# A causal convolution and an ELU feed-forward on one core: wider convolution bands, and the last output accumulators split by token block

## The chip, the cores and the metric

The kernel runs on one core of a Trainium2 chip. The metric is the time of one execution on the device in microseconds (us); the number given is the median over several executions.

## The reference

Everything is computed for 8 x 4096 = 32,768 tokens of 192 channels. First comes a causal convolution over 7 tokens with one set of softmaxed taps per head (8 heads of 24 channels), then a feed-forward block of width 2048 whose activation is ELU.

```python
w = softmax(weight)                      # (8 heads, 7 taps)
x_pad = concat([zeros(B, 6, D), x], 1)   # causal: six zeros ahead of each sequence
att[b,s,h,:] = sum_k w[h,k] * x_pad[b, s+k, head h]
h = att @ w_in                           # (32768,192) @ (192,2048)
g = where(h > 0, h, exp(min(h, 0)) - 1)  # ELU
out = g @ w_out                          # (32768,2048) @ (2048,192)
```

## The kernel before

**Tiling.** The tokens are taken in 32 superblocks of 1024 (`SUP`), each of two groups `g` of 512 tokens (`GS`). The hidden width is cut in 16 blocks `q` of 128 (`FC`). TensorE is used as two independent halves of 64 rows each: `rt = 0` holds contraction rows 0 to 63 and `rt = 1` holds rows 64 to 127 (`tile_position=(HP * rt, 0)`). The document calls them the lower and the upper half. All eight PSUM banks are one tile `H` of 8 x 512 fp32 columns, and every accumulator takes one bank.

**Three kinds of matmul.**

- *Convolution* (`"c"`, L968). The stationary operand is a band matrix `Tm` for one head, the moving operand is a window of raw x (`xg`, 240 columns: 10 windows of 24 channels). A window has 112 output tokens (`CW`), so the band is read as `Tm[rows, h, 0:CW]`, though the tile is 128 columns wide (`BW`). A superblock has 4 units `m` of two heads; each unit needs two matmuls in the lower half (64 rows) and, after those, two in the upper half (54 rows) that add to the same bank. ScalarE then copies the unit to `csb` (L735), and a DMA transpose on the SP queue (L587) makes `att`, the next superblock's moving operand.
- *First product* (`"h"`, L993). For each `q` and group three matmuls of 512 columns with `w_in` stationary fill a bank. The lower half computes group 0, the upper half group 1. The bank then goes through three engines: ScalarE writes the exp to `E` (L739), GpSimd takes the minimum with 1 (L692), and VectorE computes max(E - 1, H) and writes the fp16 block `gT` (L855). The bank is free when VectorE is done (`s_tt`).
- *Second product* (`"o"`, L1016). `gT` is stationary, 64 rows x 128 tokens, and `w_out` moves 192 columns. The accumulator for a half superblock `k` and group `g` holds two blocks `kb` of 128 tokens side by side in one bank (384 columns). The two halves of TensorE add to it in turns (`s_turn`); after the last turn (`s_fin`) ScalarE copies 384 columns to `osb` (L746), and a store of 192 KB is issued on the SP queue (L544). The very last one, `(NK - 1, 1)`, is copied by VectorE (L846) and stored from ScalarE's queue (L748).

**What sets the order.** Each engine runs one list in order. A planner in the kernel's Python (L95 to L379) writes TensorE's order before the program is built: it keeps one clock per half and adds fixed costs to it (`MM_H`, `MM_O`, `MM_C = 216.0, 82.5, 102.5` ns). A new accumulator takes the bank whose modelled `freed` time is the earliest (`take_bank`, L121). The orders of ScalarE, VectorE and of SP's stores follow from the same plan. GpSimd's order is that of the units, with two x loads per superblock (`load_x`, issue at L608) put in front of certain minima.

**The end.** After the last first product, only second products are left. The planner writes them as `tail` (L334 to L354). In a first pass (`second == 0`) the lower half works for group 0 and the upper for group 1; in the second pass they change places. Each pass goes through k = 62 and k = 63, which are the two halves of the last superblock. Both groups of k = 63 therefore end at the same time, with the last matmuls of the program.

Of the kernel before, what the change touches and what calls it, by code (L numbers as in the profile page):

```python
# [12 lines left out]
P = 128  # L13
HP = 64
FC = 128
D = 192
# [3 lines left out]
CW = 112  # L20
GS = 512
SUP = 2 * GS
# [43 lines left out]
def bass_lightweight_conv__then__act_elu_kernel(  # L66
# [18 lines left out]
    NS = NT // SUP  # L85
    SPB = S // SUP
    NP = NS * NQ
    NK = 2 * NS
    assert SPB > NXB and min(O_AT) + NB > NQ

    x_flat = x.rearrange("b s d -> (b s) d")
# [63 lines left out]
    def o_items(k, g, rt, qs, visit, first, final):  # L155


        todo = [(q, kb) for q in qs for kb in range(2)]

        def issue(i):  # L160
            q, kb = todo[i]
            take_bank(("a", k, g), rt)
            if modelled():
                t = NQ * (k // 2) + q
                clock[rt] = max(clock[rt], gt_at[t, g], turned.get((k, g), 0.0) if first and i == 0 else 0.0)
            starts, ends = first and i == 0, final and i == len(todo) - 1
            item = ("o", k, g, rt, q, kb, visit if starts else None, ends)
            plan.append((clock[rt] - AHEAD, item))
            if ends:
                visits[k, g] = visit + 1  # L170
                turned[k, g] = clock[rt] + MM_O + TURNS

        gate = lambda: visits.get((k, g), 0) == visit
        return [(MM_O, lambda i=i: issue(i), gate) for i in range(len(todo))]
# [160 lines left out]
    for second in range(2):  # L335
        for rt in range(2):
            g = rt ^ second
            k, b = divmod(NP - O_AT[g], NB)
            late = NQ - QB
            if second == 0:  # L340
                lead = TAIL - (late - QB * b)
                for kk, q0, q1, v, first in (
                    (k, QB * b, late, 2 * b, True),
                    (k + 1, 0, lead, 0, True),
                    (k, late, NQ, 2 * b, False),
                    (k + 1, lead, NQ, 0, False),
                ):
                    tail[rt] += o_items(kk, g, rt, range(q0, q1), v, first, not first)
            else:
                for kk, q0, v in ((k, QB * b, 2 * b), (k + 1, 0, 0)):  # L350
                    tail[rt] += evacuated(
                        o_items(kk, g, rt, range(q0, NQ), v + 1, True, True), kk, g
                    )
# [45 lines left out]
    with ExitStack() as stack:  # L399
# [139 lines left out]
            return att[:, 0, j, c0:c1], H[:, b, c0:c1]  # L539

        def out_group(eng, k, g):
            t, half = divmod(k, 2)
            row = SUP * t + GS * g + 2 * P * half
            eng.dma_start(  # L544
                out[row : row + 2 * P, :].rearrange("(k p) d -> p k d", p=P),
                osb[:, k % 2, g, :, :],
            ).then_inc(s_out[k % 2], 16)

        def conv_evac(W, m):

# [12 lines left out]
        def acc_of(k, g):  # L563
            return H[:, bank_of["a", k, g], :]
# [6 lines left out]
                W(s_oev[g], [a for a in act_order if a[0] == "e" and a[2] == g].index(("e", k, g)) + 1)  # L571

        def out_evac(W, k, g):
            W(s_out[k % 2], 32 * (k // 2))
            W(s_fin[g], k + 1)
            return (
                osb[:, k % 2, g, :, :].rearrange("p k d -> p (k d)"),
                acc_of(k, g)[:, 0 : 2 * D],
            )

        def transpose(eng, W, s):
# [283 lines left out]
        def _tensor(pe):  # L865
# [16 lines left out]
            for item in pe_order:  # L882
# [52 lines left out]
                elif item[0] == "d":  # L935
                    j = item[1]
                    W(s_tap, 3 if j == 2 else 2)
                    first_evacuated(W, ("t", j))
                    first_evacuated(W, ("t", 3))
                    last = KSIZE - 1 - ON_DVE[j]  # L940
                    for tap in range(last + 1):
                        for half in range(2 if j == 2 else 1):
                            c0, c1 = (GS // 2 * half, GS // 2 * (half + 1)) if j == 2 else (0, GS)
                            ins = pe.matmul(  # L944
                                H[:, bank_of[item] + half, c0:c1],
                                taps[:, tap, :],
                                xT[:, j, HALO - PAD + tap + c0 : HALO - PAD + tap + c1],
                                start=(tap == 0),
                                stop=(tap == last),
                            )  # L950
                    ins.then_inc(s_first)
                elif item[0] == "c":
                    _, m, rt, q = item
                    s, u = divmod(m, CU)
                    if m == CU:
                        W(s_band, 32)
                    for gr in range(2):
                        W(s_x[s % NXB][gr], x_need[s, gr])
                    W(s_z, z_need[s])
                    if s == NS - 1:  # L960
                        W(s_xc, 1)
                    if rt == 0:
                        wait_bank(("c", m))
                    else:
                        W(s_cswap, m + 1 - CU)
                    h = HU * u + q
                    rows = slice(HP * rt, HP + (KW - HP) * rt)
                    ins = pe.matmul(  # L968
                        H[0:CW, bank_of["c", m], 256 * q : 256 * q + UC],
                        Tm[rows, h, 0:CW],  # L970
                        xg[rows, s % NXB, :, CPH * h : CPH * (h + 1)].rearrange(
                            "p w (j i) -> p j w i", j=3
                        ),
                        start=(rt == 0 and q == 0),
                        stop=(rt == 1 and q == HU - 1),
                        tile_position=(HP * rt, 0),
                    )
                    if q == HU - 1:
                        ins.then_inc(s_cv if rt else s_cswap)
                elif item[0] == "h":  # L980
                    _, n, r, j = item
                    s, q = divmod(n, NQ)
                    if j == 0:
                        part = next(k for k in range(3) if FC * q < WCOLS[k][1])
                        W(s_w[part], 48)
                        if r == 1:
                            W(*((s_wa, 1), (s_wc, 1), (s_wa, 2))[part] if q < LATE_Q else (s_wd, 16))
                        if s:
                            W(s_att[s % 2], att_need(s))
                        wait_bank(item[:3])  # L990
                    if s == 0 and q == 0:
                        first_evacuated(W, ("d", j))
                    ins = pe.matmul(  # L993
                        H[:, bank_of[item[:3]], :],
                        w_in[HP * r : HP * (r + 1), j, FC * q : FC * (q + 1)],
                        att[HP * r : HP * (r + 1), s % 2, j, 0:GS],
                        start=(j == 0),
                        stop=(j == 2),
                        tile_position=(HP * r, 0),
                    )  # L1000
                    if j == 2:
                        ins.then_inc(s_h)
                else:
                    _, k, g, rt, q, kb, visit, ends = item
                    t, half = divmod(k, 2)
                    if ends:
                        done[k, g] = done.get((k, g), 0) + 1
                    opens = visit == 0
                    if opens:
                        wait_bank(("a", k, g))  # L1010
                    if visit is not None and not opens:
                        W(s_turn[g], turns[k, g])
                    W(s_w[2 + next(k for k in range(1, 4) if q < WOUT[k])], 16)
                    W(s_tt, tt_count(NQ * t + q, g))
                    t0 = 2 * P * half + P * kb
                    ins = pe.matmul(  # L1016
                        acc_of(k, g)[:, D * kb : D * (kb + 1)],
                        gT[HP * rt : HP * (rt + 1), t % NG3, q, g, t0 : t0 + P],
                        w_out[HP * rt : HP * (rt + 1), q, :],
                        start=opens,  # L1020
                        stop=ends and done[k, g] == visits[k, g],
                        tile_position=(HP * rt, 0),
                    )
                    if ends and done[k, g] == visits[k, g]:
                        ins.then_inc(s_fin[g])
                    elif ends:
                        ins.then_inc(s_turn[g])
                        turns[k, g] = turns[g] = turns[g] + 1

        @block.sync  # L1030
        def _sync(sy):
# [34 lines left out]
                    evacuated_by(W, *item[1:])  # L1066
                    out_group(sy, *item[1:])
            for b in range(2):
                sy.wait_ge(s_out[b], 32 * NS)


# [26 lines left out]
```

## Time and profile before

| | us |
|---|---|
| median of 4 runs | 723.87 (723.81 to 723.95) |
| the profiled execution | 723.92 |
| its span in the profile | 722.1 |
| TensorE busy (matmul) | 715.7 |
| ScalarE / GpSimd / VectorE busy | 678.0 / 669.5 / 642.7 |
| last first product starts | 708.46 |
| last second product ends | 718.08 |
| last store issued | 718.77 |

The span runs from the first to the last instruction that the profile shows; 1.8 us of the execution lie outside it. In the lists of groups, a row reads: source line, engine, operation, output<-inputs, partitions x elements, and count; then busy time in us and mean duration in ns; then idle time just before these instructions and what ended it. `PE` is a matmul, `PEld` the load of its stationary operand. For matmuls "64*112 64x240" means 64 rows by 112 columns of stationary operand, 240 moving columns. A matmul's duration (263 ns, say) is from its start to its modelled end; matmuls overlap, and the rate is read from the distance of their starts. In a timeline a row reads: start in us, length in us, what, and how many in a row. The TensorE clock granted in this run is 1.0 from end to end.

### The profile page before, as it was taken

The numbers are of one execution on the slowest core, as the hardware profiler recorded it, in microseconds if no ns is written. First come the engines' busy times: TensorE is split into PE (matmuls) and PEld (weight loads), VectorE is DVE, ScalarE is ACT, GpSimd is POOL, SyncE is SP. The second block draws the span as 40 slices with busy tenths as digits, with TensorE's granted clock in tenths as the row PEclk, the third lists the DMA queues.
The fourth block names the chain that finished last, engine by engine and source line by source line (L and its number), as shares of the span: only waits on it lengthen the run. The fifth ranks groups of instructions, "written<-read, shape, count | busy, mean of one in ns | idle before, by whom it ended". The sixth has DMA issues, their size and how long they took to land.

```text
span 722.1 us, 27608 instructions
## 1 busy us (share of the span) xinstructions
PE 715.7 (99%) x11846; PEld 677.1 (94%) x11847; DVE 642.7 (89%) x1048; ACT 678.0 (94%) x1287; POOL 669.5 (93%) x1115
## 2 busy tenths in 40 slices
PE   8999999999999999999999999999999999999997
PEld 4689999999999999999999999999999999999997
DVE  7988898998898988989888989988989988999993
ACT  6999999999999999999999999999999999999993
POOL 9999999999999999999999999999999999999893
PEclk9999999999999999999999999999999999999999
DMA  9655354555254663354553455552535553644212
GB/s 170 93 86 78 64 90 74 95 86 83 54 96 72 88 96 64 72 87 82 86 97 53 81 75 95 86 88 49 95 74 96 86 69 66 98 72 83 71 35 68
DMA packets 132703, 58.75 MB, mean 81 GB/s; under 512 B 98582, under 2 KB 132004, under 8 KB 132580
## 3 DMA queue, kind: packets, MB, share of 16 engines
q1 hardware_dynamic: 88228, 39.23, 23.8%
q0 software_dynamic: 43936, 16.77, 22.8%
q8 instruction: 93, 1.52, 0.9%
q10 hardware_dynamic: 416, 0.98, 0.4%
q14 instruction: 30, 0.25, 0.1%
HBM read 34.63 MB, written 25.46 MB: 83 GB/s over the span
## 4 chain that ended last, share of the span: by engine, by line
PE 95%; POOL 2%; ACT 1%; DVE 1%; issue 0%; DVEq 0%; POOLq 0%
PE H L1016 54%; PE H L993 38%; PE H L968 3%; DVE gT L855 1%; ACT E L739 1%; POOL w_in L628 1%; POOL xg L608 0%; POOL w_out L639 0%; ACT csb L735 0%; POOL E L692 0%; POOL owner L656 0%; DVE osb L846 0%; ACT osb L746 0%; POOL block L666 0%; POOL ident L645 0%
## 5 line engine op out<-in xcount | busy, mean ns | idle before, releaser
L855 DVE SCALAR_TENSOR_TENSOR gT<-E,H 128x512 f16<-128x512 f32 x1024 | 632.9, 682 | 64.8 <-POOL E L692 63.0
L1016 PE MATMUL H<-w_out,gT 64*128 64x192 f16 x8192 | 681.7, 243 | 0.1
L993 PE MATMUL H<-att,w_in 64*128 64x512 bf16 x3072 | 679.9, 376 | 0.5 <-DVE gT L855 0.3
L1016 PEld LDWEIGHTS H<-w_out,gT 64*128 64x128 f16 x8192 | 623.2, 94 | 23.3 <-PE H L1016 1.7
L692 POOL TENSOR_SCALAR E<-E 128x512 f32<-128x512 f32 x1024 | 607.1, 613 | 39.6 <-ACT E L739 28.5
L739 ACT ACTIVATE E<-H 128x512 f32<-128x512 f32 x1024 | 592.8, 601 | 27.1 <-PE H L993 1.6
L993 PEld LDWEIGHTS H<-att,w_in 64*128 64x128 bf16 x3072 | 275.5, 93 | 7.8 <-issue 1.2
L968 PE MATMUL H<-xg,Tm 64*112 64x240 bf16 x496 | 92.5, 266 | 0.1
L735 ACT ACTIVATE csb<-H 112x480 bf16<-112x480 f32 x124 | 70.0, 565 | 0.2
L746 ACT ACTIVATE osb<-H 128x384 f32<-128x384 f32 x127 | 61.6, 486 | 7.5 <-PE H L1016 7.4
L968 PEld LDWEIGHTS H<-xg,Tm 64*112 64x112 bf16 x496 | 57.6, 125 | 3.3 <-DVE gT L855 1.1
L608 POOL DMA_DIRECT2D xg<-in_x_dram x62 | 55.2, 893 | 0.2 <-issue 0.2
L846 DVE COPY osb<-H 128x384 f32<-128x384 f32 x1 | 0.6, 556 | 7.3 <-PE H L1016 7.3
L890 PE MATMUL H<-zw 128*128 128x512 bf16 x10 | 4.6, 627 | 1.2 <-DVE zw L754 1.2
L628 POOL DMA_DIRECT2D w_in<-in_moe_w_in_dram x9 | 5.3, 647 | 0.0
L890 PEld LDWEIGHTS H<-zw 128*128 128x128 bf16 x10 | 1.2, 135 | 2.9 <-issue 1.6
L714 ACT ACTIVATE xb<-xs 128x512 bf16<-128x512 f32 x3 | 1.7, 619 | 2.3 <-DMA xs<-in_x_dram 2.3
L944 PE MATMUL H<-xT,taps 128*128 128x256 bf16 (+1 forms) x23 | 3.7, 314 | 0.2 <-issue 0.2
L944 PEld LDWEIGHTS H<-xT,taps 128*128 128x128 bf16 x24 | 2.2, 97 | 1.5
L639 POOL DMA_DIRECT2D w_out<-in_moe_w_out_dram x3 | 2.7, 903 | 0.0
L707 ACT ACT_TABLE_LOAD x1 | 1.3, 1283 | 1.2 <-PEq L1083 1.2
L720 ACT ACTIVATE w_in<-w_in 64x1536 bf16<-64x1536 bf16 (+1 forms) x2 | 2.3, 1162 | 0.0
(43 smaller groups left out, 19.6 us busy)
## 6 DMA issues: line engine op xcount, KB each, us to landing
out_dram<-osb SPq DMA_DIRECT2D x127, 192.0 KB, 3.4
xg<-in_x_dram POOLq DMA_DIRECT2D x61, 240.0 KB, 5.0
xs<-in_x_dram ACTq DMA_DIRECT2D x1, 768.0 KB, 4.5
att<-csb SPq DMA_TRANSPOSE x31, 4.3
w_in<-in_moe_w_in_dram POOLq DMA_DIRECT2D x6, 64.0 KB, 2.9
w_in<-in_moe_w_in_dram POOLq DMA_DIRECT2D x3, 128.0 KB, 5.3
w_out<-in_moe_w_out_dram POOLq DMA_DIRECT2D x2, 192.0 KB, 9.3
w_out<-in_moe_w_out_dram POOLq DMA_DIRECT2D x1, 384.0 KB, 12.0
```

The lines of the kernel that those rows point to most:

```text
L608: g.dma_start(xg[0:rows, b, 2 * w0 + gr : 2 * w1 : 2, :], src).then_inc(s_x[b][gr], 16)
L628: g.dma_start(w_in[0:HP, j, c0:c1], bass.AP(tensor=moe_w_in.tensor, offset=8 * j * FF + c0, ap=[[CPH * FF, HEADS], [FF, 8], [1, c1 - c0]], ...
L692: g.tensor_scalar(out=E[:, i % NE, :], in0=E[:, i % NE, :], scalar1=1.0, scalar2=0.0, op0=ALU.min, op1=ALU.max,).then_inc(s_clp)
L735: a.activation(*conv_evac(W, m), ACT.Copy).then_inc(s_ce)
L739: a.activation(E[:, i % NE, :], H[:, bank_of[item], :], ACT.Exp).then_inc(s_exp)
L746: a.activation(*out_evac(W, *item[1:]), ACT.Copy).then_inc(s_oev[item[2]])
L855: v.scalar_tensor_tensor(out=gT[:, s % NG3, q, u, :], in0=E[:, i % NE, :], scalar=1.0, in1=H[:, bank_of[item], :], op0=ALU.subtract, op1=A ...
L890: pe.matmul(H[:, bank, :], zw[:, 0:P], zw[:, 0:GS], start=True, stop=True)
L944: ins = pe.matmul(H[:, bank_of[item] + half, c0:c1], taps[:, tap, :], xT[:, j, HALO - PAD + tap + c0 : HALO - PAD + tap + c1], start=(tap ...
L968: ins = pe.matmul(H[0:CW, bank_of["c", m], 256 * q : 256 * q + UC], Tm[rows, h, 0:CW], xg[rows, s % NXB, :, CPH * h : CPH * (h + 1)].rearr ...
L993: ins = pe.matmul(H[:, bank_of[item[:3]], :], w_in[HP * r : HP * (r + 1), j, FC * q : FC * (q + 1)], att[HP * r : HP * (r + 1), s % 2, j, ...
L1016: ins = pe.matmul(acc_of(k, g)[:, D * kb : D * (kb + 1)], gT[HP * rt : HP * (rt + 1), t % NG3, q, g, t0 : t0 + P], w_out[HP * rt : HP * (r ...
```

## The change

It has two parts.

1. The convolution's matmuls read the whole 128 columns of the band (`Tm[rows, h, :]`) and write 128 partitions of the bank in place of 112. The readers are unchanged.
2. The count of output accumulators `NK` is 65 in place of 64. A new function `blocks_of(k)` gives for each `k` its superblock `t`, its `half`, and its token blocks. For k < 63 that is both blocks, as before. k = 63 and k = 64 are the two blocks of the last half: each has a bank of its own (for each group), its own copy of 192 columns and its own store of 96 KB. In both passes of the tail, k + 2 follows k + 1. The accumulator that VectorE copies and ScalarE's queue stores, `(NK - 1, 1)`, is now the second block of group 1.

```diff
-    NK = 2 * NS
+    NK = 2 * NS + 1
+
+    def blocks_of(k):
+        t, half = divmod(min(k, 2 * NS - 1), 2)
+        return t, half, (range(2) if k < 2 * NS - 1 else range(k - 2 * NS + 1, k - 2 * NS + 2))
...
-        todo = [(q, kb) for q in qs for kb in range(2)]
+        todo = [(q, kb) for q in qs for kb in blocks_of(k)[2]]
...
                     (k, QB * b, late, 2 * b, True),
                     (k + 1, 0, lead, 0, True),
+                    (k + 2, 0, lead, 0, True),
                     (k, late, NQ, 2 * b, False),
                     (k + 1, lead, NQ, 0, False),
+                    (k + 2, lead, NQ, 0, False),
...
-                for kk, q0, v in ((k, QB * b, 2 * b), (k + 1, 0, 0)):
+                for kk, q0, v in ((k, QB * b, 2 * b), (k + 1, 0, 0), (k + 2, 0, 0)):
...
         def out_group(eng, k, g):
-            t, half = divmod(k, 2)
-            row = SUP * t + GS * g + 2 * P * half
+            t, half, kbs = blocks_of(k)
+            row = SUP * t + GS * g + 2 * P * half + P * kbs[0]
             eng.dma_start(
-                out[row : row + 2 * P, :].rearrange("(k p) d -> p k d", p=P),
-                osb[:, k % 2, g, :, :],
-            ).then_inc(s_out[k % 2], 16)
+                out[row : row + P * len(kbs), :].rearrange("(k p) d -> p k d", p=P),
+                osb[:, half, g, kbs[0] : kbs[-1] + 1, :],
+            ).then_inc(s_out[half], 16)
...
         def out_evac(W, k, g):
-            W(s_out[k % 2], 32 * (k // 2))
+            t, half, kbs = blocks_of(k)
+            W(s_out[half], 32 * t)
             W(s_fin[g], k + 1)
             return (
-                osb[:, k % 2, g, :, :].rearrange("p k d -> p (k d)"),
-                acc_of(k, g)[:, 0 : 2 * D],
+                osb[:, half, g, kbs[0] : kbs[-1] + 1, :].rearrange("p k d -> p (k d)"),
+                acc_of(k, g)[:, D * kbs[0] : D * (kbs[-1] + 1)],
             )
...
                     ins = pe.matmul(
-                        H[0:CW, bank_of["c", m], 256 * q : 256 * q + UC],
-                        Tm[rows, h, 0:CW],
+                        H[:, bank_of["c", m], 256 * q : 256 * q + UC],
+                        Tm[rows, h, :],
...
             for b in range(2):
-                sy.wait_ge(s_out[b], 32 * NS)
+                sy.wait_ge(s_out[b], 32 * (NS + b))
```

Outside the end, every engine's list of instructions keeps its order and its waits. In the end, TensorE has the same 225 second products in another order; ScalarE has two copies more, and the SP queue two stores more.

More of the change, by code (lines that the diff above doesn't have):

```diff
@@ L1004, in _tensor @@
                     _, k, g, rt, q, kb, visit, ends = item
-                    t, half = divmod(k, 2)
+                    t, half, _ = blocks_of(k)
                     if ends:
```

## The prediction

> **What bounds the kernel now.** First the page, for who is busy and what the end waits for; then groups by form, for the operation that is changed; then the chain and timelines inside one superblock (1024 tokens); last the end of the run.
>
> ```profile
> span 722.1 us, 27608 instructions
> PE 715.7 (99%) x11846; PEld 677.1 (94%) x11847; DVE 642.7 (89%) x1048; ACT 678.0 (94%) x1287; POOL 669.5 (93%) x1115
> ...
> PE 95%; POOL 2%; ACT 1%; DVE 1%; issue 0%; DVEq 0%; POOLq 0%
> ```
>
> TensorE sets the end. A busy TensorE is not a full one, so I set the start times in the trace against each other. In one half of the array (64 rows; rt 0 is the lower, rt 1 the upper) consecutive matmuls start 216 ns apart after an L993, 82.5 after an L1016, 102.5 after an L968. Per half and superblock that makes 48 x 215.8 + 128 x 82.5 + 8 x 102.5 = 21,738 ns. The chain shows how long a superblock takes:
>
> ```profile
> 242.52 0.25 PE H L993 x2
> 261.51 0.25 PE H L993 x2
> 262.86 0.27 PE H L993 x2
> 264.38 0.25 PE H L993 x2
> ```
>
> 264.38 - 242.52 = 21.86 us. So 0.12 us per superblock, 3.8 us over 31, is all that is not streaming: the most that any better load of weights could give in the steady part.
>
> The convolution, by form, and then the same matmuls in one stretch (253 to 264 us):
>
> ```profile
> L968 PE MATMUL H<-xg,Tm 64*112 64x240 bf16 x248 | 46.7, 268 | 0.1
> L968 PE MATMUL H<-xg,Tm 54*112 54x240 bf16 x248 | 45.8, 264 | 0.0
> L968 PEld LDWEIGHTS H<-xg,Tm 54*112 54x112 bf16 x248 | 29.4, 126 | 0.2 <-PE H L968 0.2
> ...
> L993 PEld LDWEIGHTS H<-att,w_in 64*128 64x128 bf16 x3072 | 275.5, 93 | 7.8 <-issue 1.2 <-DVE gT L855 0.9 <-ACT csb L735 0.6
> ```
> ```profile
> L968 PE MATMUL H<-xg,Tm x12: 260/263/307, 253.2 to 263.5; 64*112 64x240 bf16 x6, 54*112 54x240 bf16 x6
> ```
>
> A load of 112 columns takes 126 ns, one of 128 takes 93. But a load is seen only where it could not be fetched ahead: the median conv matmul takes 263 ns and one of twelve takes 307. That one opened a PSUM bank and waited for VectorE (s_tt); its load began when the wait ended, and its partner started 147 ns later instead of 102.5.
>
> **The change, part by part.** *1. Bands of 128 columns (496 loads, 496 matmuls).* The moving operand keeps 240 columns, so each matmul keeps its 102.5 ns; rows 112 to 127 of the result are read by nobody (L735 still reads 112).
>
> [...]The rows agree on which load is fast, not on what it is worth: bare, the narrow load costs 307 - 263 = 44 ns, and the wide one about 10 (the L1016 matmuls of this stretch have median 243 and maximum 252, L993 376 and 386). So a bare load saves 34 ns, and bare is one in sixteen: the lower half's mean of 268 against the median of 263 is 5 x 248 = 1.2 us, of which 34/44 or 1.0 us would go.
>
> Does that 1.0 us reach the end? The loop that sets the 21.86 us says no:
>
> ```profile
> 258.48 3.59 POOL L692 TENSOR_SCALAR E<-E 128x512 f32<-128x512 f32 x6
> 262.01 0.89 POOL L608 DMA_DIRECT2D xg<-in_x_dram  x1
> 262.94 1.20 POOL L692 TENSOR_SCALAR E<-E 128x512 f32<-128x512 f32 x2
> ```
> ```profile
> 258.63 4.27 DVE L855 SCALAR_TENSOR_TENSOR gT<-E,H 128x512 f16<-128x512 f32 x7
> 263.60 3.08 DVE L855 SCALAR_TENSOR_TENSOR gT<-E,H 128x512 f16<-128x512 f32 x5 [0.70 <-POOL E L692]
> ```
>
> A matmul group of the *upper* half ends at 260.72; ScalarE takes its exp (260.77 to 261.37), GpSimd its minimum (261.45 to 262.07), then issues an x load (262.01 to 262.90), then does the next minimum; VectorE, idle 0.70 us for it, ends at 264.28; and at 264.34 the upper half's L993 starts late by 40 ns. These 3.6 us hold no convolution load; the other 18.2 us are the upper half streaming. The bare load sits in the lower half at 259.96. What it saves there is waited out 1.9 us later: at 261.89 the lower half stands for the conv bank (s_ce, 36 ns late), which ScalarE frees behind the exp named above, and thus at a time that the upper half sets. On the upper half's way from 242.5 to 260.3 lie two conv pairs whose second matmul starts 107 instead of 102.5 ns after the first. I take these 4.5 ns as the narrow load's: 2 x 4.5 x 31 = 0.28 us. Start-up, where the chain goes through L968 twice (34.59, 41.41): 0 to 0.07, taken 0.03. Together **-0.31 us**; bounds 0 (the 4.5 ns belong to the 54-row operand) and -1.3 (all of it on the path).
>
> *2. The last half in two block groups (k = 63, 64).* Each half of the array issues the same 112 output matmuls after 708.53, in another order, so PE ends at 718.08 as now. Two things it waits for are new. The second block's bank was the last occupied by an accumulator that ScalarE leaves at 709.85, and it is opened about 28 slots after 708.53, at 710.8: 0.9 us of cover. If that were gone, both halves would stand behind it[...]. The gT rows are used sooner (q = 11 at 710.4 rather than 711.3), but VectorE has them by 705.8. Turns between the halves keep at least 8 slots (0.66 us). So PE: 0.
>
> The copies: ScalarE gets five in place of three, SP five stores in place of three for k >= 62, the last two lying under the matmuls of k = 64 (16 slots, 1.3 us; each issue takes 0.37 to 0.53). What remains bare is the last copy and store:
>
> ```profile
> 718.11 0.49 ACT L746 ACTIVATE osb<-H 128x384 f32<-128x384 f32 x1 [1.77 <-PE H L1016]
> 718.18 0.56 DVE L846 COPY osb<-H 128x384 f32<-128x384 f32 x1 [7.30 <-PE H L1016]
> 718.77 0.40 ACTq L544 DMA_DIRECT2D out_dram<-osb  x1
> ```
> ```profile
> GB/s 0 0 0 0 0 0 0 0 0 0 95 430 342 320 351 346 268 17 0 0 0 9 9 13 17 22 182 381 372 372 364 372 195 22 26 0 0 0 0 0
> ```
>
> (DMA rate from 715 to 722.1 in 40 slices of 0.18 us.) The last store lands at 721.59, SP sees it at 721.60, the span ends at 722.06. The copy: VectorE's 256-column copy (L840) takes 425 ns and 384 columns 556, so 1.02 ns a column and 360 for 192: -0.20. The store: issue at 718.57, and then for 96 KB neither row fits. 192 KB took 2.8 us here, beside another 192 KB, and 1.9 us at 709.9 with nothing beside it. The new last two together are one such store, but the k = 63 stores (issued near 717.2 and 717.6) come just before, and the rates of 9 to 22 GB/s at 718.7 to 719.4 and 720.8 to 721.2 are single engines that trail. In that first stretch a trailing engine ends its share of the store issued at 716.40, after a 16 KB instruction fetch that took 1.75 us from 717.01; it holds as many bytes after the change. I take the middle, 2.35: landing 720.92, so **-0.66 us** with the copy; bounds -0.2 (2.8 stays) and -1.1 (1.9).
>
> [...]
>
> Sum: -0.31 - 0.66 = -0.97. The profiled execution took 723.92 us for a span of 722.06 (1.86 around it), 0.05 over the median of 723.87. Span 721.1; **722.9 us** as a median.
>
> **The rivals.** *Loads on the path.* If TensorE's own rate and not the loop through GpSimd sets the superblock, 1.0 + 0.28 us come back in part 1: -1.94 in all, 721.9. For: only 0.12 us of 21.86 is not streaming. Against: the saved 34 ns meets the s_ce wait in the same half.
>
> *The store is not shortened.* If the trailing engine ends the run, the same bytes pass it, and only 0.1 remains of part 2: 723.5. For: the rate of 22 to 26 GB/s for 0.35 us before the end. Against: half of the last 384 KB is queued 1.3 us earlier than now.
>
> *Slower: VectorE falls behind oftener.* At 282.1 one superblock took 22.12 us in place of 21.86 (286.50 against 264.38 in the chain): GpSimd stood 0.20 us before its x load at 277.36, VectorE fell behind, and a conv opening waited 0.28 us. Two superblocks of 29 show that. The price is 0.25 us each; four more eat the gain, ten more make it 1.5 us slower. If a third of all did, 10 x 0.25 - 0.97 = +1.5: 725.4. Nothing in the change lengthens GpSimd's work; only the phase shifts.
>
> **How the numbers follow.** Main case 0.60 (722.9; own range 722.4 to 723.4), loads on the path 0.17, store not shortened 0.16, slower 0.07. The range 722.0 to 723.8 takes in the first three with their bounds. A difference under 0.2% (1.45 us) can't be told from none. Faster: the path rival and the main case's edge (0.04), 0.20 in all, since not quite all of that rival lies so far; slower 0.06, the rest of that case stopping short of it; same 0.74.
>
> **What would show it.** L968's loads at 93 to 94 ns and no conv matmul over 275: step 1's mechanism. Superblocks at 21.85 in the chain and a longer s_ce wait (about 70 ns): the loop. At 21.80 or less: the path rival. VectorE's last copy near 360 ns and the last store landing 2.2 to 2.5 us after its issue: step 2. PE's last matmul elsewhere than 9.5 us after the last L993: a wait that I excluded. The prediction is wrong if the loop is not the one named, or if the drain is set by one late engine.

## The result, and the profile after

| | before | after | predicted |
|---|---|---|---|
| median of the runs, us | 723.88 | 723.09 | 722.9 |
| ratio to before, 95% interval | | 0.9989 (0.9984 to 0.9993) | 0.9987 |
| profiled execution, us | 723.92 | 723.34 | |
| its span, us | 722.06 | 721.4 | 721.1 |
| steady superblock, us | 21.86 | 21.84 | 21.85 |
| TensorE's last matmul ends, us | 718.08 | 717.40 | 717.77 |
| last store lands after that, us | 3.51 | 3.52 | 2.85 |

The change brought 0.8 us, with an interval of 0.5 to 1.2, close to the 0.97 forecast. But the last two rows show that the sum came out well because its two terms missed in opposite directions: the bands gave 0.65 us in these profiles where 0.31 was forecast, and the split end gave nothing where 0.66 was forecast. A part of this agreement is luck. The interval also shows that a difference of 0.1% can be told from none here, where the prediction had set the limit at 0.2%.

First the page and the groups by form of the kernel after (busy time, mean ns of one, idle time ahead), and the same matmuls from 253 to 264 us (between the slashes the least, the median and the longest, in ns):

```profile
span 721.4 us, 27612 instructions
PE 714.2 (99%) x11846; PEld 674.2 (93%) x11847; DVE 642.4 (89%) x1048; ACT 678.4 (94%) x1289; POOL 669.5 (93%) x1115
```
```profile
L978 PE MATMUL H<-xg,Tm 54*128 54x240 bf16 x248 | 45.6, 263 | 0.0
L978 PE MATMUL H<-xg,Tm 64*128 64x240 bf16 x248 | 45.6, 264 | 0.2 <-DVE gT L865 0.2
L978 PEld LDWEIGHTS H<-xg,Tm 54*128 54x128 bf16 x248 | 23.0, 94 | 0.2 <-PE H L978 0.2
...
L978 PE MATMUL H<-xg,Tm x12: 260/263/272, 252.9 to 263.2; 64*128 64x240 bf16 x6, 54*128 54x240 bf16 x6
```

The load is down from 126 to 94 ns, the slowest conv matmul from 307 to 272, and the lower half's mean from 268 to 264, as step 1 said. The chain, at the same four instructions as before:

```profile
242.23 0.25 PE H L1003 x2
261.21 0.23 PE H L1003 x2
262.55 0.27 PE H L1003 x2
264.07 0.25 PE H L1003 x2
```

264.07 - 242.23 is 21.84 us, 20 ns less than before. When the same matmuls of both lists are set side by side, TensorE is 0.03 us ahead inside the first superblock (from 22 us on) and 0.67 us ahead at the last: 28 steady superblocks of 20 ns, 0.1 us in the first two, next to nothing in the last two.

The end (timeline and, below it, SP's issues of stores with least, median and longest ns; then the DMA rate from 714 to 722 us in 40 slices of 0.2 us, with the stores' number, size and median us to landing):

```profile
717.37 0.33 ACT L756 ACTIVATE osb<-H 128x192 f32<-128x192 f32 x1 [0.71 <-PE H L1026]
717.51 0.36 DVE L856 COPY osb<-H 128x192 f32<-128x192 f32 x1 [7.29 <-PE H L1026]
717.90 0.35 ACTq L553 DMA_DIRECT2D out_dram<-osb  x1
...
L553 SPq DMA_DIRECT2D out_dram<-osb x5: 373/459/2030, 715.3 to 719.0; - x5
```
```profile
GB/s 0 0 0 0 0 0 0 0 0 0 0 366 346 327 342 353 192 0 0 0 8 8 12 46 334 365 258 138 338 69 315 181 19 0 0 0 0 0 0 0
...
out_dram<-osb SPq DMA_DIRECT2D x3, 96.0 KB, 2.0
out_dram<-osb ACTq DMA_DIRECT2D x1, 96.0 KB, 2.2
```

VectorE's copy has the forecast 0.36 us. Then the plan breaks: one of SP's five issues stood for 2.03 us. It is that of the first k = 63 store, from 716.47 to 718.50, while both copies of k = 64 were done by 717.87. SP issued its last store at 719.05, 1.65 us after TensorE's end, where 0.49 was assumed; the last landing came at 720.93. The rate, with the trace's packets, tells why: of the two k = 62 stores 360 of 384 KB (480 packets of 768 B) are through by 717.42. The trace has a 16 KB instruction fetch from 716.39 to 718.12, and only from 718.10 to 718.98 do the next 16 packets come, one after another, 33 to 94 ns apart (8 to 12 GB/s in the first three slices). They are 12 KB, a sixteenth of a store, and I take them for the share of a single engine that the fetch had held.

The trace's records of the landings say the same. A store raises its semaphore in 16 single steps (1024 updates for the 64 stores with half 0), and the page counts 16 DMA engines. Of the 32 landings of the two k = 62 stores, 30 are in by 717.78; the other two come at 719.43 and 719.93, which is 1.31 and 1.81 us after the fetch has ended. Before the change it was so too: 30 by 718.46, the other two at 720.12 and 720.60, 1.35 and 1.84 us after the fetch. The rest of the landings of after are in by 720.76, so the late issue alone would have cost nearly as much as the trailing engine.

### The profile page after: what moved, and what is told of

The parts are those of the page before. It is cut to its first block, busy times and chain, and to the rows that moved or that the text cites. A ratio compares the mean times of both kernels' runs of the same rounds, so it can differ in the third digit from the quotient of the medians.

```text
span 721.4 us, 27612 instructions
## 1 busy us (share of the span) xinstructions
PE 714.2 (99%) x11846; PEld 674.2 (93%) x11847; DVE 642.4 (89%) x1048; ACT 678.4 (94%) x1289; POOL 669.5 (93%) x1115
## 3 DMA queue, kind: packets, MB, share of 16 engines
q8 instruction: 93, 1.52, 0.9%
## 4 chain that ended last, share of the span: by engine, by line
PE 95%; POOL 2%; DVE 1%; ACT 1%; issue 0%; DVEq 0%; POOLq 0%
PE H L1026 54%; PE H L1003 38%; PE H L978 4%; DVE gT L865 1%; POOL w_in L638 1%; ACT E L749 1%; POOL xg L618 0%; POOL w_out L649 0%; ACT csb L745 0%; POOL E L702 0%; POOL owner L666 0%; ACT osb L756 0%; DVE osb L856 0%; POOL block L676 0%; POOL ident L655 0%
## 5 line engine op out<-in xcount | busy, mean ns | idle before, releaser
L1026 PE MATMUL H<-w_out,gT 64*128 64x192 f16 x8192 | 681.9, 243 | 0.1
L1003 PE MATMUL H<-att,w_in 64*128 64x512 bf16 x3072 | 680.0, 376 | 0.5 <-DVE gT L865 0.3
L1026 PEld LDWEIGHTS H<-w_out,gT 64*128 64x128 f16 x8192 | 623.7, 94 | 23.8 <-PE H L1026 1.6
L1003 PEld LDWEIGHTS H<-att,w_in 64*128 64x128 bf16 x3072 | 275.5, 93 | 7.8 <-issue 1.2
L978 PE MATMUL H<-xg,Tm 64*128 64x240 bf16 x496 | 91.2, 263 | 0.2 <-DVE gT L865 0.2
L756 ACT ACTIVATE osb<-H 128x384 f32<-128x384 f32 (+1 forms) x129 | 62.3, 485 | 6.8 <-PE H L1026 6.8
L978 PEld LDWEIGHTS H<-xg,Tm 64*128 64x128 bf16 x496 | 43.7, 94 | 4.8 <-DVE gT L865 1.1
L926 PE MATMUL H<-ident,xb 64*64 64x64 bf16 x48 | 1.7, 243 | 0.8 <-ACT xb L724 0.8
```

The source lines that it names most:

```text
L756: a.activation(*out_evac(W, *item[1:]), ACT.Copy).then_inc(s_oev[item[2]])
L978: ins = pe.matmul(H[:, bank_of["c", m], 256 * q : 256 * q + UC], Tm[rows, h, :], xg[rows, s % NXB, :, CPH * h : CPH * (h + 1)].rearrange(" ...
L1003: ins = pe.matmul(H[:, bank_of[item[:3]], :], w_in[HP * r : HP * (r + 1), j, FC * q : FC * (q + 1)], att[HP * r : HP * (r + 1), s % 2, j, ...
L1026: ins = pe.matmul(acc_of(k, g)[:, D * kb : D * (kb + 1)], gT[HP * rt : HP * (rt + 1), t % NG3, q, g, t0 : t0 + P], w_out[HP * rt : HP * (r ...
```

## The experiments

The start-up (first loads) differs between executions: the first of the first products starts at 12.19 to 12.91 us in these profiles. So the bands are judged from superblock to superblock and the end from TensorE's last matmul on; times are given with their intervals, as ratios to before on the same chip (its median there was 723.86 or 723.87, and 724.47 for the four kernels with the fetch moved or heads cut). A ratio is estimated from all runs and need not equal the quotient of the two medians. Each kernel has one profile.

### One part alone

The bands alone (kernel before):

```diff
-                        H[0:CW, bank_of["c", m], 256 * q : 256 * q + UC],
-                        Tm[rows, h, 0:CW],
+                        H[:, bank_of["c", m], 256 * q : 256 * q + UC],
+                        Tm[rows, h, :],
```

> The kernel before with the wide bands alone; the end is as before. Theory now: the whole gain is here, because the end gained nothing: the last second product ends 0.7 us earlier than before, superblocks take 21.84 us, and the time is 0.7 us under before (ratio 0.9990). As predicted on record: 0.31 us under before, superblocks at 21.85. Rival, that the split end does pay and something else in it hides the gain: about 0.3 us under before.

Measured: 723.59, ratio 0.9996 (0.9988 to 1.0004); superblocks of 21.844; 0.49 us gained from the first superblock to the last; last landing 3.34 us after TensorE's end.

The split end alone is the kernel after with those two lines as they were:

> The kernel before with the split end alone, bands of 112 columns. Theory now: the SP queue stands about 2 us in the issue of the third store of the end, behind one DMA engine that is held by a 16 KB instruction fetch, so the last store lands no sooner after the last matmul than before: time within 0.15 us of before. As predicted on record: 0.66 us under before, with the last issue 0.5 us after the last matmul. If the standing of 2 us in the changed kernel was an accident of that run: 0.5 to 0.7 us under before.

Measured: 723.71, ratio 0.9999 (0.9991 to 1.0007); superblocks of 21.86, 0.02 us gained over all of them; last landing 3.01 us after TensorE's end. Here too an SP issue stood, for less long:

```profile
L553 SPq DMA_DIRECT2D out_dram<-osb x5: 373/431/1519, 716.3 to 719.5; - x5
```

So the steady gain is the bands' alone, and it is larger than forecast. (TensorE ends 0.3 us later than before here, for the start-up took longer.) The end's gain isn't a fixed number: 0.50 us in this profile, none in the profile after, with the same instructions in it. The times alone are too wide to divide 0.8 us between the parts.

### Which half's load counts

I had put the gain in the upper half (4.5 ns at two pairs) and had written off the lower half's bare load. So the wide bands went into the lower half only, with the end as before:

```diff
-                        H[0:CW, bank_of["c", m], 256 * q : 256 * q + UC],
-                        Tm[rows, h, 0:CW],
+                        H[0 : P if rt == 0 else CW, bank_of["c", m], 256 * q : 256 * q + UC],
+                        Tm[rows, h, 0 : P if rt == 0 else CW],
```

> The kernel before, with wide bands in the lower half alone (rt = 0); the upper half keeps 112 columns. Theory now: what counts is the one bare load per superblock, which is in the lower half, so this gives the whole gain of the bands: superblocks at 21.84 us, 0.6 to 0.7 us under before. As predicted on record, with the gain in the upper half's 4.5 ns per pair: nothing in the steady part, superblocks stay at 21.86, 0 to 0.1 us under before.

Measured: 723.43, ratio 0.9991 (0.9983 to 0.9999); superblocks of 21.840; 0.64 us gained. The lower half alone brings all of it. (The upper half alone was not tried.) In the kernel after, the second matmul of the upper half's pairs still starts 107 ns after the first: the 4.5 ns are not the narrow load's.

How the lower half's time gets through is seen in ScalarE's timeline from 260.4 to 261.3: two exps, of which the second is the upper half's, the one that the prediction's loop begins with. Before, after, and lower half only:

```profile
260.13 1.24 ACT L739 ACTIVATE E<-H 128x512 f32<-128x512 f32 x2
```
```profile
259.84 1.22 ACT L749 ACTIVATE E<-H 128x512 f32<-128x512 f32 x2
```
```profile
260.28 1.22 ACT L739 ACTIVATE E<-H 128x512 f32<-128x512 f32 x2
```

The pair takes 20 ns less from first start to last end. In single records: the upper half's last matmul of that group to the start of its exp is 433 ns before, and 412 after and with the lower half only. At 21 of the 31 other groups of a superblock it is 412 to 415 ns in before, too; it is over 420 at the rest.

Where the 21 ns arise is in the trace's records of semaphore updates. Most L993 tell their end 390 ns after their start, most L1016 256 or 257 ns after. At that place the lower half's last L1016 of a turn stands ahead of the upper half's L993 in TensorE's list. Start, end as told, and (for the upper half) the end that was due, in us:

| | lower half's L1016: start, told | upper half's L993: start, due, told | told apart, ns |
|---|---|---|---|
| before | 260.459, 260.716 | 260.339, 260.729, 260.750 | 34 |
| after | 260.137, 260.394 | 260.049, 260.439, 260.439 | 45 |
| lower half only | 260.577, 260.833 | 260.490, 260.879, 260.879 | 46 |

(L1016 and L993 are L1026 and L1003 in the kernel after.) Two things hold for all 3304 matmuls of before that tell their end: the ends are told in the order of the list, though in 242 places a matmul starts ahead of its forerunner there, and never less than 34 ns apart (34 or 35 ns in 712 cases). In before the upper half's end was due 13 ns behind the lower half's, so it was told 21 ns late, and with it came ScalarE, GpSimd, the x load and VectorE. The other superblocks show the same: in 28 of the last 30 superblocks of before the two are 34 or 35 ns apart at this place, and the upper half's end is 19 ns late in the median. In the profiles with wide bands, in both halves or in the lower one, the medians are 38 to 48 ns apart, and at most two superblocks of the 30 have a late end. What can be gained at this place is no more than those 20 ns.

### Less and more work in the lower half

If only the time of the lower half matters, other ways to shorten it should give the same 20 ns, and no more. In the kernel before, one head (or both) of unit 2 convolves 160 instead of 240 columns, in both halves; this leaves out a third of the head's columns of that unit, so the result is incomplete and only the time is of use:

```diff
+                    nj = 2 if u == 2 and q in (1,) else 3
...
-                        H[0:CW, bank_of["c", m], 256 * q : 256 * q + UC],
+                        H[0:CW, bank_of["c", m], 256 * q : 256 * q + 80 * nj],
...
-                        ),
+                        )[:, 0:nj],
```

> The kernel before with bands of 112 columns; only the third convolution unit's second head takes 160 moving columns rather than 240 in both halves, so one sixth of that unit is left out of the result. After the bare load the lower half is 33 ns earlier, as much as a wide load gives, with no wide load. If what counts is the lower half's lateness there: superblocks at 21.84 us. If wide loads act in another way (the load port, the other half's loads): superblocks stay at 21.86.

> As the run beside it, with both heads of the third unit at 160 columns: the lower half is 67 ns earlier. If the two halves' completion signals came too close together there (the exp of the next upper unit starts 433 ns after its last matmul's start in the kernel before, 412 in the changed one and everywhere else), 33 ns are enough to part them and 67 give no more: superblocks at 21.84, exp at 412. If the lower half's time lies on the loop in proportion: 21.82.

Measured: one head, 33 ns less: 723.67, ratio 0.9989 (0.9983 to 0.9996), superblocks of 21.846, exp 413 ns after its matmul. Both heads, 67 ns less: 723.62, ratio 0.9983 (0.9973 to 0.9993), superblocks of 21.845, exp 413 ns. The chains of the two:

```profile
242.20 0.25 PE H L994 x2
...
264.04 0.25 PE H L994 x2
```
```profile
242.51 0.25 PE H L994 x2
...
264.36 0.25 PE H L994 x2
```

Twice the saving gives no more: the two ends are told 39 and 73 ns apart (medians of the superblocks), both over 34, and the gain is the same. What is beyond it is waited out, as the prediction had said of the whole, and so is what the upper half saves of its own. The 4 to 6 ns between 21.846 and 21.840 stay unexplained.

Then the other way: two 16-column matmuls more behind unit 2's pair in the lower half, into columns that nobody reads:

```diff
+                    if u == 2 and rt == 0 and q == HU - 1:
+                        for e in range(HU):
+                            ins = pe.matmul(
+                                H[0:CW, bank_of["c", m], 256 * e + UC : 256 * (e + 1)],
+                                Tm[rows, h, 0:CW],
+                                xg[rows, s % NXB, 0, 0 : 256 - UC],
+                                start=False,
+                                stop=False,
+                                tile_position=(HP * rt, 0),
+                            )
```

> The kernel before with bands of 112 columns, and two more matmuls of 16 columns in the lower half after the third unit's two (they write columns that nobody reads): the lower half is 20 to 60 ns later at the place of the bare load. The upper unit's exp starts 433 ns after its last matmul's start in the kernel before. If a matmul of one half can't signal its end before the matmuls ahead of it in the list, which are the other half's, have ended: the 433 grows by the whole delay, and so does the superblock: 21.88 to 21.92. If it is only two signals that come too close together: they are parted the other way round, 412 and superblocks at 21.84. The 62 more matmuls move TensorE's last instruction fetch about 2.5 us earlier, so the end is not to be compared.

Measured: 725.85, ratio 1.0035 (1.0022 to 1.0049).

```profile
243.13 0.25 PE H L1003 x2
...
265.08 0.25 PE H L1003 x2
...
L980 PE MATMUL H<-xg,Tm 64*112 64x16 bf16 x62 | 6.8, 181 | 0.0
```

The lower half is 80 ns later at that place and the superblock is 85 ns longer (21.945). The exp again follows its matmul by 412 ns (the two ends are told 44 ns apart), so this run doesn't repeat the late signal; instead the upper half's own second L1003 started 314 ns after the first rather than 216, behind the lower half's small matmuls in TensorE's list. Neither expectation had this. What can be kept: lateness in the lower half does reach the end, here through a start and not through a signal.

### What the stores wait for

Two theories for the issue that stood: a queue holds only so many stores in flight, or every queue stands while one DMA engine is held by the fetch. So two of the last stores go from ScalarE's queue:

```diff
+    BY_ACT = ((NK - 3, 1), (NK - 2, 1))
...
+                    if item[1:] in BY_ACT:
+                        evacuated_by(W, *item[1:])
+                        out_group(a, *item[1:])
...
-                elif item[1:] != (NK - 1, 1):
+                elif item[1:] != (NK - 1, 1) and item[1:] not in BY_ACT:
```

> The changed kernel, with the group 1 stores of k = 62 and 63 issued from ScalarE's queue rather than SP's, so that each queue issues three stores in turn at the end. Theory now: a queue's third store stands because two stores of 192 KB are still unread by the held DMA engine; with 192 + 96 KB ahead of it the third goes out at once. No issue above 0.6 us, last issue about 0.5 us after the last matmul, last landing 2.1 to 2.5 us after it, time 0.4 to 0.7 us under the changed kernel (ratio to before 0.9980 to 0.9985). Rival, that the held DMA engine itself ends the run whatever the queue: all issues short, but the landing as late as in the changed kernel, and the time equal to it. Second rival, that every queue stands while the engine is held: an issue of 1.5 to 2 us remains on SP or ScalarE.

Measured: 723.22, ratio 0.9993 (0.9984 to 1.0001); last landing 3.29 us after TensorE's end.

```profile
L554 SPq DMA_DIRECT2D out_dram<-osb x3: 344/345/372, 715.7 to 719.1; - x3
L554 ACTq DMA_DIRECT2D out_dram<-osb x3: 398/413/1525, 716.1 to 718.8; - x3
```

SP is free of it, and ScalarE stands 1.53 us (717.21 to 718.73) instead; the fetch ended at 718.29. Worse, ScalarE's copy for k = 64 stood behind its own issue. A limit of SP's queue doesn't explain that; a held engine fits it, though no record shows the engine. Why it comes one store later than in the kernel after is open.

The next runs move the fetch itself. A shorter warm-up ahead of the loop, with 24 small matmuls in it, puts 44 more instructions ahead of the main work, so that each fetch should fall that much earlier in it. This was run with the split end and with the end of before (bands wide in both):

```diff
-WARM = (6, 1, 4)
+WARM = (6, 1, 2)
+TINY = 24
...
+                    for _ in range(TINY if item[2] == WARM[2] else 0):
+                        pe.matmul(H[:, bank, 0:HP], zw[:, 0:P], zw[:, 0:HP], start=True, stop=True)
```

> The changed kernel, with the last two of the ten warm-up matmuls of 512 columns taken out and 24 of 64 columns put in their place. That puts 44 more instructions ahead in TensorE's list, so its last 16 KB instruction fetch should come about 1 us earlier, before the stores of the end. Theory now: the held DMA engine ends the run (in the six profiles so far the last store lands 2.66 to 2.84 us after that fetch ends), so with the fetch out of the way no issue stands for over 0.6 us, and the last landing is 2.3 to 2.6 us after the last matmul's end instead of 3.5: 0.9 us under the changed kernel, ratio to before about 0.998. Rival, that four or five stores so close together are slow of themselves: an issue still stands 1.5 us or more, landing 3.3 us or more after the last matmul, time that of the changed kernel.

> Wide bands with the end as before, and the same warm-up as in the run beside it: the undivided end without the fetch. Theory now: landing 2.9 to 3.0 us after the last matmul's end instead of 3.3 to 3.6. [...]

Measured: split end 722.75, ratio 0.9981 (0.9971 to 0.9990), landing 2.45 us after TensorE's end; end of before 723.18, ratio 0.9987 (0.9979 to 0.9995), landing 3.00. The stores of k >= 62 by size and median us to landing, split end and then old end:

```profile
out_dram<-osb SPq DMA_DIRECT2D x3, 96.0 KB, 1.8
out_dram<-osb ACTq DMA_DIRECT2D x1, 96.0 KB, 1.7
```
```profile
out_dram<-osb SPq DMA_DIRECT2D x3, 192.0 KB, 2.3
out_dram<-osb ACTq DMA_DIRECT2D x1, 192.0 KB, 2.3
```

One part of the expectation failed: that with the fetch out of the way no issue stands for over 0.6 us. With the split end it was SP's issue of the second k = 62 store:

```profile
L554 SPq DMA_DIRECT2D out_dram<-osb x5: 373/461/1207, 715.8 to 718.5; - x5
```

With the old end the same issue stood for 1.00 us. In all five profiles with such an issue it ended 0.24 to 0.44 us after the fetch. Here it stands early enough to leave the last stores alone.

All profiles together except the last version's, from the fetch's records, in us from TensorE's end:

| kernel | fetch starts | fetch ends | last landing | landing - fetch end |
|---|---|---|---|---|
| before | -1.06 | 0.69 | 3.51 | 2.82 |
| bands alone | -1.12 | 0.52 | 3.34 | 2.82 |
| after | -1.02 | 0.72 | 3.52 | 2.81 |
| split end alone | -1.07 | 0.35 | 3.01 | 2.66 |
| lower half only | -0.93 | 0.80 | 3.61 | 2.81 |
| stores on two queues | -1.03 | 0.46 | 3.29 | 2.84 |
| one head cut | 0.10 | 1.06 | 3.88 | 2.82 |
| two heads cut | -0.24 | 0.81 | 3.63 | 2.82 |
| fetch moved, old end | -2.06 | -1.08 | 3.00 | |
| fetch moved, split end | -1.85 | -0.85 | 2.45 | |
| two matmuls more | -3.51 | -2.20 | 3.01 | |

In all eight profiles in which the fetch ends after TensorE, the last landing comes 2.66 to 2.84 us after the fetch, old end or split. In each of them 30 of the 32 landings of the k = 62 stores are in by the end of the fetch (0.03 us after it at the latest), and the last two come 1.17 to 1.35 and 1.66 to 1.84 us after it. Where the fetch ends 0.85 us or more before TensorE, no such pair trails, and the last landing is at 3.00 and 3.01 with the old form and 2.45 with the split one. So the split end is worth 0.55 us between these profiles, once the fetch is out of the way (the medians are 0.43 apart).

The count of instructions isn't all that places the fetch: with heads cut it starts 0.8 to 1.2 us later than in before, though TensorE's list is as long. Why is open.

### A version with all of these

Wide bands, split end, stores on both queues, and the fetch moved a little further (TINY = 34):

```diff
+TINY = 34
```

> The changed kernel with the stores of the end on both queues in turn and 34 matmuls of 64 columns in the warm-up: the last instruction fetch about 1.4 us earlier than in the changed kernel. Theory: no store of the end stands for over 0.6 us, the last landing comes 2.2 to 2.4 us after the last matmul's end (2.45 with the fetch alone moved, 3.5 in the changed kernel); 0 to 0.2 us under that run, ratio to before 0.998. If the landing has reached what two last stores of 96 KB take by themselves: no difference from it.

Measured: 722.32 against 723.87, ratio 0.9983 (0.9976 to 0.9989); the fetch ends 1.13 us before TensorE, and the last landing comes 2.21 us after TensorE's end. No issue stands (first view), and the rate has no single engine that trails (second view, the same slices of 0.2 us as above):

```profile
L555 SPq DMA_DIRECT2D out_dram<-osb x3: 345/345/373, 715.8 to 718.2; - x3
L555 ACTq DMA_DIRECT2D out_dram<-osb x3: 339/345/398, 716.2 to 718.4; - x3
```
```profile
GB/s 0 0 0 0 0 0 0 0 82 0 0 0 0 161 342 357 354 372 323 192 357 369 116 8 0 219 361 350 54 0 0 0 0 0 0 0 0 0 0 41
```

It is faster than before. Against the kernel after it has the shorter end, but the intervals of the two ratios, from different chips, overlap. Whether its last 0.24 us (2.45 to 2.21) are from the two queues or from the fetch moved further was not tested.

## Why the prediction was right in its sum and wrong in its parts

*Part 1, mechanism: right.* Loads of 94 ns, no conv matmul over 273 ns in the whole run, 33 ns saved at the one bare load in the lower half: as forecast. The trace has loads of 126 ns before and 94 after. By estimate from these two that is 32 ns x 248 = 7.9 us for a half if all were bare; 0.65 us came, since only bare loads counted here, as the prediction's rows had it.

*Part 1, size: the step that failed* is "What it saves there is waited out 1.9 us later", with its reason "These 3.6 us hold no convolution load ... at a time that the upper half sets". The s_ce wait did grow, but from 36 to 47 ns, not to 70. The loop's first event, the upper half's exp, was itself late by 21 ns because of the lower half, whose end was told only 34 ns earlier; the runs with only the lower half's bands and with the cut heads show that this is what the bands removed. I had taken the exp's start from one place in the trace of before and not compared it with the same distance elsewhere: 433 against 412 ns would have shown it. 28 x 20 ns is 0.56 us that the prediction had put at nothing.

*Part 1, the 4.5 ns: wrong.* The second matmul of the upper half's pairs starts at 107 ns with either width. This term of 0.28 us was nothing; the lower of its bounds, that the 4.5 ns have another cause, was the right end. The two errors (0.28 too much, some 0.6 too little) partly cancel, and so the part's sum of 0.31 is off by only 0.34 from the measured 0.65.

*Part 2, TensorE and copies: right.* PE ends where the bands leave it, no half waits for the new bank, and VectorE's copy is 356 ns against 360. That both halves would stand behind such a wait can be seen in before: where the lower half's conv opening waited until 282.08, the upper half's L993 behind it in the list started at 282.09, 325 ns after its forerunner instead of 216.

*Part 2, stores: wrong.* "Each issue takes 0.37 to 0.53" failed: one took 2.03. The "2.35" to landing was between two rows; the last store needed 1.88 us from its issue, but was issued 1.16 us later than assumed, which together gives 0.69 more and eats the 0.66. The rival "The store is not shortened" had it: the same bytes pass the one engine that trails. I had read the fetch and its trailing engine in the trace of before, and yet applied them only to the first stretch. The row was there: before ends 2.82 us after its fetch. With the fetch away the part is worth 0.55, near the 0.66 of the rows. That the whole came to 0.8 against 0.97 owes much to luck: the end's gain was lost to the fetch, and the bands' gain that was not forecast made up for half of it.

*The rivals.* "Loads on the path" (21.80 us per superblock or less) did not come: the gain stops at 20 ns, however much the lower half saves. "VectorE falls behind oftener" did not come either: the same two long superblocks are in both profiles (22.10 and 22.12 us before, 22.09 and 22.09 after), and no other.

*What is open.* Why the last fetch takes 1.4 to 1.75 us in six of the eight profiles, when the median of the 93 fetches of before is 0.98; and why it comes when it does. The last version's end is 1.31 us shorter than that of after in its profile, but its median is only 0.77 us less: in that profile TensorE's last matmul ends 0.47 us later (717.87), after a later start. Whether the new warm-up or chance makes that start late was not tested.

## What to carry to other kernels

Take the distance from a matmul to its reader at every place where it occurs, before calling a loop independent of another stream: an odd one (433 among 412, with the reader free) says that something is late. A saving in work that ends beside the critical path can pass on a part (here 20 ns of 33 or of 67), up to the point where the two ends are apart (here 34 ns), and no more. And before the last stores are made smaller, see whether an instruction fetch falls on them: here the last landing came 2.66 to 2.84 us after it with stores of 192 KB and of 96, and 44 instructions more ahead of it moved it by 0.8 to 1.0 us.

## What was not expected of the hardware

- A 16 KB instruction fetch near the end set the end: last landing 2.66 to 2.84 us after it in eight profiles. Two landings of the k = 62 stores trail it in each, 0.49 us apart. As an estimate from these rows: the last four stores of before, 768 KB, are 48 KB for each of 16 engines. One engine that takes up its 12 KB of the first when the fetch is over, has it landed 1.35 us later, and needs 0.49 us for each of the other three, ends at 2.82 us, as measured. The trace does not name the engine of a landing, so that it is one and the same is inferred.
- In five profiles the issue of a store stood until 0.24 to 0.44 us after the fetch, on SP (2.03, 1.52, 1.21 and 1.00 us) or on ScalarE (1.53 us), and with it all that the engine had queued behind. That it waits for the DMA engine held by the fetch is inferred.
- The halves of the array weren't independent here. All 3304 ends that before tells come in the list's order and at least 34 ns apart, and one half's end, due 13 ns behind the other's, was told 21 ns late. And behind two small matmuls in one half the other's next start came 98 ns late (314 ns after the first instead of 216).
